# A hand-ordered attention and gMLP kernel: 50 steps of its list in other places, twelve of them zero products of the warm-up

## The chip, the cores and the metric

The kernel runs on one core of a Trainium2 chip. The core has five queues that work side by side and are each strictly in order here: TensorE (PE in the profile, its weight loads PEld), VectorE (DVE), ScalarE (ACT), GpSimd (POOL) and SyncE (SP), which issues nearly all DMAs. The metric is the device time of one execution in microseconds (us); lower is better.

## The reference

Inputs are q, k and v of shape (8, 8, 576, 64): 8 batches, 8 heads, 576 positions, head size 64. First comes attention with a causal window of 64 positions, then a gMLP block with spatial gating on the heads laid side by side.

```
scores = q @ k^T / 8 ; keep 0 <= t - s < 64, else -1e9
attn   = softmax(scores) ; x = (attn @ v) as (8, 576, 512)
h      = relu(x @ w_in)                 # 512 -> 1024
u, v   = h[..., :512], h[..., 512:]
v_n    = (v - mean(v)) / sqrt(var(v) + 1e-6)
v_s    = w_spatial @ v_n + b_spatial    # over the 576 positions
out    = (u * v_s) @ w_out              # 512 -> 512
```

## The kernel before, in words

All work is cut into 1111 named steps. A plan is first built: each step has a name, the engine that may run it, the buffers that it takes and the instructions that it issues. Then the string ORDER at the top of the file says in which order the steps are emitted, on which engine, and which buffer of its kind each one takes: `S0_0:PE:0:1` is step S0_0 on TensorE with score tiles 0 and 1. The function `as_listed` reads it, and the last loop of the kernel emits it. Since every engine's queue is in order, the places in ORDER are the order of each queue; across engines only semaphores for data and buffers hold a step back. A step that takes a buffer waits until the last readers of the step that had it are done.

The names, with b a batch, g a half of the heads (0 or 1), u a quarter, j or i a block of rows or columns:

- ldk, ldq, ldv (L401, L422), ldwin (L327), ldwsp (L343), ldb, ldwo: loads, issued by SyncE (DQ in the list). Loads of v come in five pieces (ldv2_03 is piece 3 of batch 2, half 0). There are 8 buffers for k, q and weights ("nat") and 4 for v ("natv").
- ck, cq, cv, sl, su, s4, cwin, cwsp, cb, cwo: casts to 16 bits and copies (L293 on ScalarE, L296, L299 and L301 on VectorE and GpSimd).
- tk, tq: 32 x 32 transposes on VectorE (L408).
- S (64 small matmuls, L470; S*_r, the last 64 positions, L539): scores into the two score tiles. Each S takes both. E (L477, L549): their exponential on ScalarE. M (L480, L553): the window's mask, a minimum on VectorE.
- Z (L493, L562): row sums; N and n (L519, L521): their logarithm and its negative exponential on ScalarE, so the inverse. P (L504, L575): attn @ v. X (L512, L583): product of both on VectorE, which gives x.
- V (L653, L666): the half of h that is normalised; Vr (L633) its relu, Vb (L635) and Va (L637) its statistics on VectorE, L1 and L2 (L680, L682) on ScalarE, A (L692) the normalised v_n on VectorE.
- U (L708, L713) and Ur (L721): the other half and its relu. W and We: transposes of w_spatial through TensorE, once, which need all five ldwsp.
- G (L738, L744) and Ge (L752): spatial product and gate. O (L763, and L669 within V*_4 of the next batch): product with w_out. Oe (L610): copy out of PSUM on ScalarE. st (L619, L626 and others): stores, in SyncE's queue too.
- D0 to D24 (L791): 25 steps of two matmuls each of a zeroed tile with itself into a bank that nobody reads. They have no data to wait for after the tile has been zeroed.

```
for _ in range(2):
    nc.tensor.matmul(m.t[:, :], scratch[:, 0:128], scratch[:, :], start=True, stop=True)
add(f"D{i}", ("PE", 0.43), -2.0, emit_D, acq=[m], mode="f")
```

TensorE has two score tiles of two PSUM banks each and four single banks, 0 to 3, which all other matmul steps take. The batches overlap: while the gMLP of batch b runs, the attention of batch b + 1 and the loads of b + 2 and b + 3 are under way. Before the first S stand eight D steps; the other 17 lie between the steps of the first attention, up to P0_11.

Of the kernel before, what the change touches and what calls it, by code (L numbers as in the profile page):

```python
# [42 lines left out]
Ur0_0:ACT:4 cv1_01:POOL W3:PE:1 We0:DVE ldv1_14:DQ sl1_00:ACT:2 We2:DVE ldk2_1:DQ:4 W4:PE:0
s41_0:ACT su1_00:DVE We3:ACT sl1_01:POOL W1:PE:2 su1_01:POOL A0_2:DVE:2 We4:ACT Z1_r:PE:3 P1_01:PE:1
A0_1:DVE:3 N1_r:ACT:0 We1:DVE ck2_0:POOL:0 ldwo10:DQ:5 P1_00:PE:0 Z1_10:PE:3 X1_00:DVE:2 G0_4:PE:2
ldq2_1:DQ:7 N1_10:ACT:4 G0_3:PE:0 n1_01:ACT X1_01:DVE tk2_0:DVE:2 cv1_10:POOL:3 ldwo00:DQ:6
n1_10:ACT sl1_10:ACT:3 G0_0:PE:3 su1_10:POOL cq2_0:ACT:1 ldwo11:DQ Ge0_3:DVE:0 G0_2:PE:1 ldwo01:DQ
Ge0_4:DVE:1 tq2_0:DVE:3 cv1_11:POOL ldq3_0:DQ:0 G0_1:PE:0 ldv2_00:DQ:0 s41_1:POOL sl1_11:ACT
su1_11:POOL n1_r:ACT Ge0_2:DVE:2 P1_10:PE:2 n1_11:ACT X1_10:DVE:3 ck2_1:POOL:2 P1_11:PE:1
ldk3_0:DQ:2 S2_0:PE:1:0 X1_11:DVE cwo10:ACT ldv2_01:DQ P1_r:PE:2 Ge0_0:DVE:3 V1_2:PE:1 E2_00:ACT:0  # L50
X1_r:DVE:1 Ge0_1:DVE:4 E2_01:ACT:1 V1_1:PE:3 cq2_1:POOL:3 ldv2_02:DQ tk2_1:DVE:0 V1_3:PE:2
Vr1_2:ACT:5 ldv2_03:DQ cwo00:POOL Vr1_1:ACT:6 tq2_1:DVE:1 U1_2:PE:0 ldv2_10:DQ:1 Vr1_3:ACT:7
cwo11:ACT ldv2_11:DQ V1_0:PE:1 M2_00:DVE Ur1_2:ACT:5 Vb1_2:DVE:5 cwo01:ACT S2_1:PE:1:0 Vr1_0:ACT:4
M2_01:DVE Z2_00:PE:3 cq3_0:POOL:0 ldv2_04:DQ E2_10:ACT:3 V1_4:PE:2 Vb1_1:DVE:1 ldv2_12:DQ Va1_2:DVE
Vb1_3:DVE:3 U1_1:PE:0 Vr1_4:ACT:2 M2_10:DVE Oe0_4:ACT:0 O0_0:PE:1 ck3_0:POOL:1 ldv2_13:DQ
Vb1_4:DVE:0 E2_11:ACT:2 Vb1_0:DVE:2 ldq4_0:DQ:3 O0_2:PE:2 Oe0_0:ACT:0 Va1_3:DVE ldv2_14:DQ Va1_4:DVE
Va1_1:DVE Ur1_1:ACT:0 Va1_0:DVE S2_r:PE:1:0 M2_11:DVE Z2_10:PE:1 cv2_00:POOL:1 ldv3_00:DQ:2
L11:ACT:1 O0_1:PE:0 tq3_0:DVE:4 L21:ACT Oe0_2:ACT:1 ldq3_1:DQ:1 N2_10:ACT:3 U1_4:PE:2 ldk3_1:DQ:4
A1_4:DVE E2_r0:ACT:0 U1_0:PE:1 N2_00:ACT:5 A1_0:DVE:4 ldv5_10:DQ:3 A1_2:DVE:5 Ur1_4:ACT:3 A1_1:DVE:6
U1_3:PE:3 Oe0_1:ACT A1_3:DVE:7 sl2_00:ACT:0 su2_00:POOL tk3_0:DVE:5 G1_1:PE:2 Ur1_3:ACT:1  # L60
# [13 lines left out]
O1_3:PE:0 n3_00:ACT ldk4_1:DQ:6 sl3_00:POOL:3 ldv4_00:DQ:1 Oe1_2:ACT:1 Va2_4:DVE Va2_2:DVE Va2_1:DVE
U2_1:PE:3 tk4_0:DVE:0 Ur2_3:ACT:1 su3_00:POOL L12:ACT:0 O1_0:PE:2 L22:ACT Oe1_3:ACT A2_4:DVE
s43_0:POOL A2_1:DVE:0 Ur2_1:ACT:3 O1_1:PE:1 ldv4_10:DQ:2 A2_3:DVE:1 s43_1:ACT ldk5_0:DQ:0 A2_0:DVE:2
Oe1_0:ACT:0 Z3_10:PE:0 A2_2:DVE:3 ldv4_11:DQ P3_00:PE:3 N3_10:ACT:3 P3_10:PE:2 ldq5_0:DQ:2
X3_00:DVE:2 S4_0:PE:1:0 ldv4_01:DQ Oe1_1:ACT M3_r:DVE ldv4_02:DQ G2_4:PE:0 ck4_1:ACT:0 ldv4_03:DQ
G2_2:PE:3 ldv5_11:DQ Ge2_4:DVE:1 E4_00:ACT:0 ldv4_04:DQ tk4_1:DVE:1 G2_3:PE:1 E4_01:ACT:3
ck5_0:POOL:1 ldk5_1:DQ:1 Ge2_2:DVE:0 ldv4_12:DQ Z3_11:PE:0 n3_10:ACT Ge2_3:DVE:2 Z3_r:PE:3  # L80
S4_1:PE:1:0 N3_r:ACT:4 X3_10:DVE:3 N3_11:ACT:2 P3_11:PE:1 M4_01:DVE n3_r:ACT P3_01:PE:3 cq5_0:POOL:3
ldv4_13:DQ P3_r:PE:2 n3_11:ACT G2_0:PE:0 X3_r:DVE:1 E4_10:ACT:2 ldq5_1:DQ:3 X3_01:DVE st1_1:DQ
X3_11:DVE G2_1:PE:2 E4_11:ACT:1 Ge2_0:DVE:3 ldv5_00:DQ:0 V3_3:PE:3 ldv5_01:DQ Ge2_1:DVE:4 st1_0:DQ
M4_00:DVE V3_1:PE:1 Vr3_3:ACT:5 M4_10:DVE Z4_01:PE:0 Vr3_1:ACT:6 M4_11:DVE V3_4:PE:2 ck5_1:POOL:2
N4_01:ACT:1 tk5_0:DVE:4 Z4_10:PE:3 Vr3_4:ACT:7 Z4_00:PE:1 S4_r:PE:1:0 Oe2_4:ACT:0 V3_2:PE:0
cv4_00:POOL:1 Vb3_1:DVE:2 N4_10:ACT:0 Vb3_3:DVE:4 U3_0:PE:2 E4_r0:ACT:0 sl4_00:POOL:0 Vr3_2:ACT:4
N4_00:ACT:3 U3_2:PE:3 Vb3_2:DVE:5 cq5_1:POOL:0 Ur3_0:ACT:5 tq5_0:DVE:5 V3_0:PE:0 su4_00:ACT
s44_0:POOL U3_4:PE:1 Va3_2:DVE cv4_10:POOL:0 Vr3_0:ACT:2 ldv6_10:DQ:1 O2_2:PE:2 ldv5_12:DQ
Ur3_2:ACT:4 Vb3_0:DVE:1 ldv4_14:DQ Ur3_4:ACT:2 U3_1:PE:0 Vb3_4:DVE:0 ldv5_02:DQ E4_r1:ACT
Oe2_2:ACT:1 ldv5_03:DQ Va3_3:DVE Va3_0:DVE P4_01:PE:3 Va3_1:DVE Va3_4:DVE ldq6_1:DQ:4 M4_r:DVE  # L90
# [751 lines left out]
```

## Time and profile before

| what | value |
|---|---|
| runs, us | 202.72, 202.97, 202.5 (median 202.72) |
| span of the profiled execution | 201.0 us |
| the profiled execution's own time beside its span | not given apart from the runs |
| TensorE busy | 188.6 us, 94% |
| VectorE, ScalarE, GpSimd busy | 161.2, 167.0, 76.5 us |
| mean granted TensorE clock | 0.996 |
| DMA | 42.69 MB, 212 GB/s on average |

A row of the timeline has its start, its length (of several instructions of one kind in a row, to the end of the last), engine, line, operation, destination and sources, shapes and count; in brackets the idle time ahead of it and what ended that. A row of the chain of waits has start, length and what the end of the program hung on at that time. A row of the windows has the stretch, its length, then the busy time of TensorE, its weight loads, VectorE, ScalarE and GpSimd with the number of instructions, the granted clock, the DMA engines' share and GB/s.

### The profile page before, as it was taken

The numbers are of one execution on the slowest core, as the hardware profiler recorded it, in microseconds if no ns is written. First come the engines' busy times: TensorE is split into PE (matmuls) and PEld (weight loads), VectorE is DVE, ScalarE is ACT, GpSimd is POOL, SyncE is SP. The second block draws the span as 40 slices with busy tenths as digits, with TensorE's granted clock in tenths as the row PEclk, the third lists the DMA queues.
The fourth block names the chain that finished last, engine by engine and source line by source line (L and its number), as shares of the span: only waits on it lengthen the run. The fifth ranks groups of instructions, "written<-read, shape, count | busy, mean of one in ns | idle before, by whom it ended". The sixth has DMA issues, their size and how long they took to land.

```text
span 201.0 us, 7008 instructions
## 1 busy us (share of the span) xinstructions
PE 188.6 (94%) x2927; PEld 97.7 (49%) x2927; DVE 161.2 (80%) x307; ACT 167.0 (83%) x307; POOL 76.5 (38%) x144
## 2 busy tenths in 40 slices
...
GB/s 221 387 276 184 336 378 210 292 372 377 185 274 255 246 221 188 295 243 234 311 118 262 241 316 178 227 284 249 185 111 117 3 5 132 108 0 0 128 145 202
DMA packets 50275, 42.69 MB, mean 212 GB/s; under 512 B 39361, under 2 KB 39489, under 8 KB 50242
## 3 DMA queue, kind: packets, MB, share of 16 engines
...
q8 instruction: 23, 0.38, 0.8%
q10 hardware_dynamic: 224, 0.33, 0.5%
...
## 4 chain that ended last, share of the span: by engine, by line
PE 70%; DMA 9%; SPq 7%; ACT 5%; DVE 5%; POOL 1%; issue 1%; POOLq 0%
PE bank L738 16%; PE bank L653 12%; PE bank L763 12%; PE bank L708 10%; DMA nk<-in_k_dram 9%; SPq L422 4%; PE pair L470 4%; PE bank L504 3%; PE bank L666 3%; PE bank L493 3%; PE bank L744 2%; SPq L327 2%; ACT e L477 1%; PE bank L713 1%; ACT ob L610 1%
## 5 line engine op out<-in xcount | busy, mean ns | idle before, releaser
L738 PE MATMUL bank<-wspT,vn 128*128 128x512 f16 (+1 forms) x160 | 37.5, 379 | 0.0
L477 ACT ACTIVATE e<-pair 128x1024 f16<-128x1024 f32 x32 | 31.9, 1027 | 2.7 <-PE pair L470 2.5
L752 DVE TENSOR_TENSOR g<-bank,ru 128x512 f16<-128x512 f32 (+1 forms) x40 | 24.8, 632 | 11.0 <-PE bank L738 5.0
L708 PE MATMUL bank<-x,win 128*128 128x512 f16 x128 | 31.6, 379 | 0.0
L763 PE MATMUL bank<-wout,g 128*128 128x512 f16 x128 | 31.3, 379 | 0.0
L653 PE MATMUL bank<-win,x 128*128 128x512 f16 x128 | 30.4, 379 | 0.2 <-DVE x L512 0.2
L721 ACT ACTIVATE ru<-bank 128x512 f32<-128x512 f32 (+1 forms) x40 | 21.4, 562 | 8.4 <-PE bank L708 4.6
L635 DVE BATCH_NORM_STATS2 st<-vs 128x6 f32<-128x512 f16 (+1 forms) x40 | 25.9, 670 | 3.0 <-ACT vs L633 2.8
L512 DVE TENSOR_TENSOR x<-bank,lz 128x512 f16<-128x512 f32 x32 | 21.2, 683 | 5.4 <-PE bank L504 2.6
L633 ACT ACTIVATE vs<-bank 128x512 f16<-128x512 f32 (+1 forms) x40 | 22.9, 597 | 3.1 <-PE bank L653 2.3
L610 ACT COPY ob<-bank 128x512 f32<-128x512 f32 (+1 forms) x39 | 22.6, 588 | 3.3 <-PE bank L763 3.1
L738 PEld LDWEIGHTS <-vn 128*128 128x128 f16 (+1 forms) x160 | 14.9, 97 | 17.7 <-DVE vn L692 0.5
L480 DVE TENSOR_TENSOR e<-e,mask 128x1024 f16<-128x1024 f16 x32 | 22.5, 721 | 1.0 <-ACT e L477 1.0
L408 DVE STREAM_TRANSPOSE qT<-hq 128x576 f32<-128x576 f32 x16 | 19.7, 1243 | 2.5 <-POOL hq L296 2.3
L296 POOL CAST hq<-nq 128x384 f16<-128x384 f32 x33 | 16.5, 536 | 13.1 <-DMA nq<-in_q_dram 12.5
L408 DVE STREAM_TRANSPOSE kT<-hk 128x576 f32<-128x576 f32 x16 | 20.0, 1247 | 1.4 <-ACT hk L293 1.1
L519 ACT ACTIVATE lz<-bank 128x512 f32<-128x512 f32 x32 | 18.6, 603 | 2.1 <-PE bank L493 2.0
L521 ACT ACTIVATE lz<-lz 128x512 f32<-128x512 f32 x32 | 19.6, 631 | 0.1
L653 PEld LDWEIGHTS <-x 128*128 128x128 f16 x128 | 12.0, 97 | 14.3 <-issue 0.6
L708 PEld LDWEIGHTS <-win 128*128 128x128 f16 x128 | 11.9, 98 | 14.4 <-issue 1.3
L763 PEld LDWEIGHTS <-g 128*128 128x128 f16 x128 | 11.8, 98 | 13.4 <-issue 0.5
L692 DVE TENSOR_SCALAR vn<-vs,mv,ln 128x512 f16<-128x512 f16 (+1 forms) x40 | 15.4, 436 | 3.5 <-ACT ln L682 3.3
...
## 6 DMA issues: line engine op xcount, KB each, us to landing
...
```

What stands on the lines that cost most here:

```text
L408: d = add(f"t{name}{b}_{g}", ("DVE", 1.09), key, lambda e: nc.vector.transpose(qt.t[:, :].rearrange("p (i j) -> p j i", j=18), h.t[:, :].b ...
L477: ex = add(f"E{b}_{g}{u}", ("ACT", 0.91), key, lambda e, u=u: nc.scalar.activation(e2[u].t[:, :, :], sc[u].t[:, :, :], AF.Exp, bias=0.0, s ...
L480: mins.append(add(f"M{b}_{g}{u}", ("DVE", 0.65), key, lambda e, u=u: nc.vector.tensor_tensor(e2[u].t[:, :, :], e2[u].t[:, :, :], mask[:, : ...
L610: lambda e: (nc.vector.tensor_copy if last else nc.scalar.copy)(view(), m.t[rows, 0:n]),
L633: rl = add(f"Vr{b}_{j}", ("ACT", 0.49), key, lambda e: nc.scalar.activation(vs.t[0:jn, :], m.t[0:jn, :], AF.Relu), deps=[pv], acq=[vs], us ...
L635: s1 = add(f"Vb{b}_{j}", ("DVE", 0.6), key + 0.02, lambda e: nc.vector.bn_stats(st6.t[0:jn, 0:6], vs.t[0:jn, :]), deps=[rl], acq=[st6], us ...
L653: nc.tensor.matmul(m.t[:, :], xr(b, r)[:, 128 * j:128 * j + 128], w_in_sb[r][:, 512:1024], start=(r == 0), stop=(r == 3))
L708: nc.tensor.matmul(m.t[:, :], w_in_sb[r][:, 128 * i:128 * i + 128], xr(b, r), start=(r == 0), stop=(r == 3))
L721: lambda e, m=m, ru=ru, n=n: nc.scalar.activation(ru.t[:, 0:n], m.t[:, 0:n], AF.Relu), deps=[pu], acq=[ru], uses=[m])))
L738: nc.tensor.matmul(m.t[:, :], w[0:kn, 128 * i:128 * i + 128], wspT[kk][0:kn, 0:512], start=(kk == 0), stop=(kk == 4))
L752: lambda e, m=m, g=g, ru=ru, n=n: nc.vector.tensor_tensor(g.t[:, 0:n], m.t[:, 0:n], ru.t[:, 0:n], ALU.mult),
L763: nc.tensor.matmul(m.t[:, :], G[r][0].t[:, 128 * j:128 * j + 128], w_out_sb[r][:, :], start=(r == 0), stop=(r == 3))
```

## The change

The steps are the same, each on the same engine; 50 of them stand in other places, and the numbers of banks and buffers are dealt out anew along the list.

- TensorE: 19 D steps instead of 8 stand ahead of S0_0. D24, D13 and D19 come between S0_0 and S0_1 (before: D21, D7, D11, D24), D2, D4 and D3 between S0_1 and S0_r (before: five), and none behind S0_r (before: eight). All but the first four use bank 0. Z1_10 goes ahead of P1_00, P2_00 behind S3_0, P3_10 ahead of Z3_10, V3_0 ahead of U3_2, Z4_r ahead of P4_00, and G3_4 from behind P4_r to ahead of Z4_11.
- VectorE: Va0_1 goes from behind Va0_3 to ahead of tq1_1; Vb0_4 ahead of Va0_3; M2_11 from ahead of tq3_0 to behind tk3_0; M2_r ahead of X2_00; Va3_3 and Va3_1 ahead of Vb3_0; Ge3_4 from behind X4_11 to ahead of Ge3_1; Va4_2 ahead of Va4_4.
- ScalarE: Oe0_1, Vr3_0, Ur3_1 (now behind L23), Oe2_3, sl4_10 and n4_r (now ahead of Ur3_3), sl6_10, n5_10 and N2_01.
- GpSimd: cv2_10 ahead of su2_00, cq4_1 ahead of cq4_0, s43_0 ahead of su3_00.
- Transfers: ldwsp4 ahead of ldwsp1; ldv2_03 and ldv2_04 behind ldv2_13; ldq4_0 later and ldq4_1 earlier; ldv5_10 from ahead of ldv3_10 to ahead of st1_4; st0_1 from ahead of st0_4 to behind ldv3_04; ldv5_11, ldv4_13 later; ldv6_00 and ldv6_11 around st2_4.
- Buffers: ldv3_10 takes v buffer 3 instead of 0, ldv5_10 buffer 0 instead of 3; ldwsp4 takes nat buffer 6, ldwsp1 buffer 2, ldwsp0 buffer 0 (before: 0, 6, 2).

The core of the diff, its first hunk; the rest of ORDER changes in the same way, and since bank numbers follow, nearly every line of it does.

```diff
-ldk1_0:DQ:5 ldv0_10:DQ:1 D15:PE:3 cq0_0:POOL:0 ldv0_11:DQ D22:PE:0 D6:PE:1 tq0_0:DVE:0 D0:PE:2
-ck0_0:ACT:1 ldv0_01:DQ D16:PE:3 tk0_0:DVE:1 ck0_1:ACT:2 ldv0_02:DQ S0_0:PE:0:1 tk0_1:DVE:2 D21:PE:0
-E0_00:ACT:0 ldv0_12:DQ D7:PE:1 D11:PE:2 cq0_1:DVE:3 E0_01:ACT:1 ldv0_03:DQ D24:PE:3 tq0_1:DVE:3
-M0_01:DVE cq1_0:ACT:0 ldwin100:DQ:6 S0_1:PE:0:1 M0_00:DVE D5:PE:0 E0_10:ACT:2 tq1_0:DVE:4 D17:PE:1
-D2:PE:2 ldv0_04:DQ E0_11:ACT:3 D4:PE:3 ck1_0:DVE:1 ldv0_13:DQ D1:PE:0 S0_r:PE:0:1 M0_10:DVE
-ldv0_14:DQ Z0_00:PE:1 E0_r0:ACT:0 cv0_10:DVE:0 Z0_10:PE:2 E0_r1:ACT M0_11:DVE ldwin110:DQ:7
-Z0_01:PE:3 N0_10:ACT:0 D10:PE:0 sl0_10:DVE:0 cv0_00:DVE:1 N0_01:ACT:1 ldb:DQ:0 M0_r:DVE N0_00:ACT:2
-sl0_00:DVE:1 Z0_r:PE:2 su0_00:DVE ldwin111:DQ Z0_11:PE:0 N0_r:ACT:3 D9:PE:3 n0_00:ACT cv0_01:DVE
-ldwin101:DQ D8:PE:1 su0_01:DVE sl0_01:POOL n0_10:ACT su0_10:DVE D13:PE:2 ldwin000:DQ:1 n0_01:ACT
-tk1_0:DVE:5 s40_0:POOL ldk1_1:DQ:2 N0_11:ACT:4 P0_01:PE:3 ldq1_1:DQ:3 P0_00:PE:1 n0_11:ACT
-cv0_11:DVE ldwin001:DQ S1_0:PE:0:1 sl0_11:DVE X0_00:DVE:0 D20:PE:2 cwin110:POOL ldwin010:DQ:4
-E1_00:ACT:1 s40_1:DVE D19:PE:0 ldwin011:DQ su0_11:POOL X0_01:DVE ldwsp3:DQ:5 E1_01:ACT:0 M1_00:DVE
-cwin111:POOL P0_10:PE:1 P0_11:PE:2 X0_10:DVE:1 D18:PE:0 cwin100:ACT cwin101:POOL ldwsp2:DQ:7 D3:PE:3
-n0_r:ACT X0_11:DVE cwin000:ACT Z1_00:PE:1 M1_01:DVE ldwsp1:DQ:6 P0_r:PE:0 cb:ACT V0_1:PE:3
-X0_r:DVE:0 V0_2:PE:2 ck1_1:POOL:2 ldwsp4:DQ:0 Vr0_1:ACT:0 N1_00:ACT:5 Vb0_1:DVE:0 V0_0:PE:0
-Vr0_2:ACT:1 tk1_1:DVE:0 cq1_1:POOL:3 ldv1_00:DQ:2 V0_3:PE:3 Vr0_0:ACT:2 n1_00:ACT ldwsp0:DQ:2
-Z1_01:PE:1 tq1_1:DVE:1 V0_4:PE:2 cwin001:ACT cwin010:POOL ldv1_01:DQ N1_01:ACT:2 cwin011:POOL
+ldk1_0:DQ:5 ldv0_10:DQ:1 D15:PE:3 cq0_0:POOL:0 ldv0_11:DQ D22:PE:0 D6:PE:0 tq0_0:DVE:0 D0:PE:0
+ck0_0:ACT:1 D9:PE:0 ldv0_01:DQ D16:PE:0 tk0_0:DVE:1 D1:PE:0 D17:PE:0 ck0_1:ACT:2 ldv0_02:DQ D7:PE:0
+D11:PE:0 D18:PE:0 D5:PE:0 tk0_1:DVE:2 D10:PE:0 D21:PE:0 D8:PE:0 D20:PE:0 S0_0:PE:0:1 E0_00:ACT:0
+ldv0_12:DQ cq0_1:DVE:3 E0_01:ACT:1 ldv0_03:DQ D24:PE:0 tq0_1:DVE:3 M0_01:DVE cq1_0:ACT:0 D13:PE:0
+ldwin100:DQ:6 D19:PE:0 S0_1:PE:0:1 M0_00:DVE E0_10:ACT:2 tq1_0:DVE:4 D2:PE:0 ldv0_04:DQ E0_11:ACT:3
+D4:PE:0 D3:PE:0 ck1_0:DVE:3 ldv0_13:DQ S0_r:PE:0:1 M0_10:DVE ldv0_14:DQ Z0_00:PE:0 E0_r0:ACT:0
+cv0_10:DVE:0 Z0_10:PE:1 E0_r1:ACT M0_11:DVE ldwin110:DQ:7 Z0_01:PE:2 N0_10:ACT:0 sl0_10:DVE:0
+cv0_00:DVE:1 N0_01:ACT:1 ldb:DQ:0 M0_r:DVE N0_00:ACT:2 sl0_00:DVE:1 Z0_r:PE:3 su0_00:DVE ldwin111:DQ
+Z0_11:PE:1 N0_r:ACT:3 n0_00:ACT cv0_01:DVE ldwin101:DQ su0_01:DVE sl0_01:POOL n0_10:ACT su0_10:DVE
+ldwin000:DQ:1 n0_01:ACT tk1_0:DVE:5 s40_0:POOL ldk1_1:DQ:2 N0_11:ACT:4 P0_01:PE:2 ldq1_1:DQ:3
+P0_00:PE:0 n0_11:ACT cv0_11:DVE ldwin001:DQ S1_0:PE:0:1 sl0_11:DVE X0_00:DVE:0 cwin110:POOL
+ldwin010:DQ:4 E1_00:ACT:1 s40_1:DVE ldwin011:DQ su0_11:POOL X0_01:DVE ldwsp3:DQ:5 E1_01:ACT:0
+M1_00:DVE cwin111:POOL P0_10:PE:3 P0_11:PE:1 X0_10:DVE:1 cwin100:ACT cwin101:POOL ldwsp2:DQ:7
+ck1_1:POOL:1 ldwsp4:DQ:6 n0_r:ACT X0_11:DVE cwin000:ACT Z1_00:PE:0 M1_01:DVE ldwsp1:DQ:2 P0_r:PE:2
+cb:ACT V0_1:PE:3 X0_r:DVE:0 V0_2:PE:1 Vr0_1:ACT:0 N1_00:ACT:5 Vb0_1:DVE:0 V0_0:PE:2 Vr0_2:ACT:1
+tk1_1:DVE:0 cq1_1:POOL:2 ldv1_00:DQ:2 Va0_1:DVE V0_3:PE:3 Vr0_0:ACT:2 n1_00:ACT ldwsp0:DQ:0
+Z1_01:PE:0 tq1_1:DVE:1 V0_4:PE:1 cwin001:ACT cwin010:POOL ldv1_01:DQ N1_01:ACT:2 cwin011:POOL
 Vr0_3:ACT:3 ldv1_02:DQ Vb0_2:DVE:1 S1_1:PE:0:1 Vr0_4:ACT:4 Vb0_0:DVE:2 cwsp3:POOL ldv1_03:DQ
...
-E2_r1:ACT ldv3_10:DQ:0 Ge1_0:DVE:6 s42_1:ACT P2_00:PE:1 Z2_11:PE:2 su2_10:POOL ldv3_11:DQ
-V2_1:PE:0 cv3_10:POOL:2 Oe0_3:ACT Vb2_0:DVE:4 P2_r:PE:2 st0_1:DQ Vr2_1:ACT:2 Z3_00:PE:1 X2_r:DVE:0
+Ge1_1:DVE:5 n2_00:ACT sl2_10:POOL:1 s42_0:ACT Z2_01:PE:0 E2_r1:ACT ldv3_10:DQ:3 Ge1_0:DVE:6
+su3_10:POOL ldv3_03:DQ E3_10:ACT:3 ldv3_14:DQ G1_2:PE:2 ldv3_04:DQ ck4_0:POOL:1 tq4_0:DVE:3 st0_1:DQ
...
```

More of the change, by code (lines that the diff above doesn't have):

```diff
@@ L43 @@
[L43 to L60, printed above, removed]
@@ L73 @@
-Ur2_4:ACT:4 cv3_00:POOL:3 Oe1_4:ACT:0 O1_2:PE:2 Vb2_2:DVE:0 n3_01:ACT st1_4:DQ Va2_3:DVE Vb2_4:DVE:1
[L74 to L90, printed above, removed]
@@ L91 @@
-Ur3_1:ACT:1 P4_00:PE:1 tq5_1:DVE:0 ldv5_13:DQ S5_0:PE:1:0 L13:ACT:1 n4_00:ACT Z4_r:PE:2 L23:ACT
-O2_0:PE:0 N4_r:ACT:4 A3_3:DVE:4 n4_01:ACT X4_00:DVE:0 O2_1:PE:2 E5_01:ACT:3 A3_0:DVE:5 A3_1:DVE:6
-A3_4:DVE U3_3:PE:1 Oe2_0:ACT:0 A3_2:DVE:7 Oe2_1:ACT M5_01:DVE O2_3:PE:0 E5_00:ACT:0 X4_01:DVE
-G3_0:PE:2 tk5_1:DVE:1 Ur3_3:ACT:0 n4_10:ACT G3_3:PE:3 M5_00:DVE n4_r:ACT Oe2_3:ACT sl4_10:ACT:1
-su4_10:POOL G3_1:PE:1 Ge3_3:DVE:8 Ge3_0:DVE:5 s44_1:POOL Z4_11:PE:0 Z5_01:PE:3 Ge3_1:DVE:6
-cv5_00:POOL:2 ldv6_00:DQ:2 N4_11:ACT:5 P4_10:PE:2 S5_1:PE:0:1 ldv5_04:DQ X4_10:DVE:1 N5_01:ACT:2
```

171 lines of the change are left out of this document (106 added, 65 removed).

## The prediction

> **What bounds the kernel now.** I read the page first, then the chain that ended last, then the timeline of the first 31 us engine by engine, then windows, because most moved steps lie early. No separate time is given for the profiled execution: its span is 201.0 us and the median of the three runs is 202.72 us (202.5 to 202.97). The 1.7 us between them are taken as fixed, and every change below is added to 202.72. A difference of 0.2% is 0.4 us, about what a measurement of this kernel can tell from none.
>
> ```profile
> span 201.0 us, 7008 instructions
> PE 188.6 (94%) x2927; PEld 97.7 (49%) x2927; DVE 161.2 (80%) x307; ACT 167.0 (83%) x307; POOL 76.5 (38%) x144
> ```
>
> ```profile
> 19.27 6.71 DMA nk<-in_k_dram
> 26.10 1.41 POOL hk L296 x3
> 27.51 1.39 POOL hq L296 x3
> 28.92 1.27 DVE qT L408
> 30.23 0.81 PE pair L470 x46
> ```
>
> ```profile
> 39.91 0.76 PE bank L744 x20
> ```
>
> TensorE is busy 94% of the span, and from 40 us on the chain is nearly all TensorE. So a delay that reaches G0_4 at 39.91 is carried to the end unless TensorE later gives back a stall. The chain's early part is a load (ldk1_1, issued at 19.27), its casts on GpSimd, a transpose on VectorE (tq1_1) and S1_1 at 30.23. Here the zero products matter only by what waits behind them.
>
> ```profile
> 1.27 5.35 PE L791 MATMUL bank<-scratch 128*128 128x512 f16 x16 [1.27 <-DVE scratch L234]
> 8.67 0.76 PE L470 MATMUL pair<-qT,kT 32*64 32x128 f16 x64 [2.05 <-DVE kT L408]
> 9.37 1.90 PE L791 MATMUL bank<-scratch 128*128 128x512 f16 x8
> 9.48 1.94 ACT L477 ACTIVATE e<-pair 128x1024 f16<-128x1024 f32 x2 [0.52 <-PE pair L470]
> 10.88 1.26 DVE L408 STREAM_TRANSPOSE qT<-hq 128x576 f32<-128x576 f32 x1
> 11.99 1.26 DVE L480 TENSOR_TENSOR e<-e,mask 128x1024 f16<-128x1024 f16 x2
> 12.20 0.77 PE L470 MATMUL pair<-qT,kT 32*64 32x128 f16 x64 [0.93 <-DVE qT L408]
> 20.49 0.77 PE L470 MATMUL pair<-qT,kT 32*64 32x128 f16 x64 [0.57 <-DVE kT L408]
> ```
>
> ```profile
> L791 PE MATMUL bank<-scratch x50: 379/379/634, 1.3 to 23.4; 128*128 128x512 f16 x50
> ```
>
> ```profile
> 12.00:25.60 13.60, 11.93 (x277) 6.25 (x278) 13.47 (x27) 11.34 (x20) 3.68 (x6) 1.00 0.95 254
> ```
>
> The reader should see two things. Before S0_0 TensorE is free for 2.05 us; and from 12.0 to 25.6 VectorE is busy 13.47 of 13.60 us, so in that stretch VectorE has no slack, while TensorE has plenty.
>
> **Part 1: eleven more zero products ahead of S0_0.** Before, eight D steps (16 matmuls, two each) stand ahead of S0_0 and end at 1.27 + 5.35 = 6.62. Now 19 stand there, 38 matmuls. The 22 more run at the pace of the x8 row: (1.90 - 0.38) / 7 = 0.217 us each, where 0.38 is the median of one such matmul (379 ns in the row of L791); 22 x 0.217 = 4.77. The last of them is out of the way at 6.62 - 0.38 + 4.77 + 0.217 = 11.2, against S0_0's 8.67: 2.5 us late. Bounds: all 38 at 0.217 would give 9.5; all at the mean pace of the first 16 (5.35 / 16 = 0.33) would give 14.0. I take 11.2, because the first 16 hold whatever the slow start costs.
>
> E0_00 and E0_01 follow S0_0 by 0.81 (9.48 - 8.67) and take 1.94, so they end at 13.95 instead of 11.42. M0_01 needs them; it started at 11.99, straight behind tq0_1, and now starts at about 14.0. That is 2.0 us late on VectorE, whose queue is in order: tq1_0, ck1_0, all cv, sl and su copies of batch 0, X0_* and M1_* stand behind it, and there is no idle time to take it up before 25.6. S0_1 needs the same score tiles and starts at 14.0, 1.8 late. The eight D steps that stood behind S0_r free nothing: P0_01, S1_0 and Z1_00 waited for VectorE and GpSimd, not for them.
>
> ```profile
> 24.57 0.62 ACT L293 CAST win<-wi 128x512 f16<-128x512 f32 x1 [0.50 <-DMA wi<-in_moe_w_in_dram]
> 25.21 0.67 ACT L293 CAST wspT<-wsb 1x576 f16<-1x576 f32 x1
> 25.91 0.60 ACT L633 ACTIVATE vs<-bank 128x512 f16<-128x512 f32 x1
> 25.22 0.41 DVE L583 TENSOR_TENSOR x<-bank,lz_r 128x256 f16<-128x256 f32 x1
> 26.54 0.69 DVE L635 BATCH_NORM_STATS2 st<-vs 128x6 f32<-128x512 f16 x1 [0.90 <-ACT vs L633]
> 27.54 1.26 DVE L408 STREAM_TRANSPOSE kT<-hk 128x576 f32<-128x576 f32 x1 [0.31 <-POOL hk L296]
> 28.92 1.26 DVE L408 STREAM_TRANSPOSE qT<-hq 128x576 f32<-128x576 f32 x1
> ```
>
> Between X0_r and tq1_1 VectorE has its first idle time: 0.90 + 0.31 + 0.12 (28.92 - 28.80). The last two wait for the casts at 26.10 and 27.51, which hang on a load that does not move. The 0.90 waits for Vr0_1 on ScalarE, which was held by cwin000's DMA wait (0.50) and cb. ScalarE is 1.85 late there, less that 0.50: Vr0_1 ends at 27.85 instead of 26.51. X0_r ends at 27.63, Vb0_1 starts at 27.85, and with tk1_1, Va0_1 (moved in ahead of tq1_1, about 0.1) and tq1_1 (31.05 instead of 30.18) 0.85 is left of the 2.0. The later queue no longer holds Va0_1, so M1_11 and all behind it, to We1 and G0_4, are **0.75 us late**. ldwsp4 and ldwsp1 change places and SyncE now stands at ldwsp1 until ck1_1 has been cast (27.51); behind it wait ldv1_00 and ldwsp0, which have some time in hand. Taken at nothing: W0, which needs all five ldwsp, is itself 0.75 later. If that cover is gone it costs some tenths.
>
> **Part 2: the clock.** With no D step behind S0_r, TensorE is nearly idle from about 16 to 26 us. The rows that come nearest:
>
> ```profile
> 18.44:21.85 3.41, 2.84 (x104) 1.74 (x102) 3.36 (x8) 2.88 (x6) 1.87 (x4) 1.00 0.86 274
> 195.93:199.35 3.42, 1.17 (x11) 0.46 (x9) 0.42 (x1) 0.96 (x2) 0.00 (x0) 1.00 0.82 293
> 199.00:200.98 1.98, 0.00 (x0) 0.00 (x0) 0.00 (x0) 0.00 (x0) 0.00 (x0) 0.59 0.20 49
> ```
>
> At the end the granted clock fell to half: a mean of 0.59 over 1.98 us is 0.36 us at full and the rest at half, so the fall came at 199.36, after 3.4 us in which TensorE was busy 1.17. In the kernel before, the stretch of that length from 18.44 holds 2.84 busy and keeps the clock. Without its zero products that stretch holds Z0_r, Z0_11, P0_01 and P0_00 alone, some 0.9 to 1.2 us, like the one that lost the clock. The other end is the 2.05 us idle before S0_0, which did not lose it; the longest single gap would now be about 1.5 us. I put the fall at a little over one half. Its price: S1_0, whose 0.70 issue time would double, delays E1_00 and through it M1_00 on the full VectorE queue: **+0.7**. The least is 0; the most is that V0_1 to V0_4 run at half too (four groups of 0.86, half hidden by the late VectorE): +2.0. I take +0.7, as S1_0's own row has it.
>
> [...]
>
> **Part 3: the loads of 57 to 78 us.**
>
> ```profile
> 57.48 5.84 SPq L422 DMA_DIRECT2D nv<-in_v_dram  x4
> 71.41 0.39 SPq L626 DMA_DIRECT2D out_dram<-ob  x1
> ```
>
> ```profile
> 78.62 5.78 DMA nk<-in_k_dram
> 87.44 0.30 PE bank L562 x4
> ```
>
> ```profile
> 86.47 0.41 PE L493 MATMUL bank<-e,ones 128*64 128x512 f16 x2
> 82.88 0.58 ACT L610 COPY ob<-bank 128x512 f32<-128x512 f32 x1
> 84.42 1.15 ACT L293 CAST hk<-nk 128x1152 f16<-128x1152 f32 x1 [0.96 <-DMA nk<-in_k_dram]
> ```
>
> The largest stall of TensorE after 40 us is here: Z3_11 at 86.47 needs 0.22, Z3_r starts at 87.44, so 0.75 is lost. Z3_r's bank waits for Ge2_2, that stands on VectorE behind tk4_1, that waits for ck4_1, and that for ldk4_1, which lands 5.78 us after its issue. In the order of before, SyncE stood twice: four issues (ldv5_10 and the first three of ldv3_1) spread over the 5.84 us from 57.48, since ldv3_10's buffer was still read, and then it stood at st0_1, which waits for Oe0_3, until 71.41. So ldv3_02 to ldv3_04 and st0_0 came after 72, not long ahead of ldk4_1. Now ldv3_10 takes another buffer and st0_1 stands behind the loads: the queue is empty when ldk4_1 is issued. If it lands 1 us sooner, ck4_1 starts when ScalarE is free (Oe1_1 ended at 83.46, plus the delay) and the 0.75 is given back. Bounds: 0 to 0.96; I take **-0.75**. ldv2_03 and ldv2_04 go behind four other loads, which makes cv2_00 1.5 us later on GpSimd; su2_10, moved behind su2_00, then ends about 1 us later, as P2_10 does: nothing.
>
> **Part 4: the rest.** M2_11, M2_r, Va and Vr moves, V3_0 ahead of U3_2, Z4_r, P3_10, P2_00, Z1_10, the GpSimd swaps and Ur3_1 behind L23: around nearly all of them TensorE has no gap, so they can gain nothing there. G3_4 ahead of Z4_11 adds Ge3_4 and a later Ur3_3 ahead of Ge3_1 and X4_10:
>
> ```profile
> 60.00:70.00 10.00, 10.00 (x188) 5.53 (x187) 8.93 (x15) 9.14 (x17) 4.10 (x9) 1.00 0.86 250
> 90.00:100.00 10.00, 10.00 (x98) 4.72 (x97) 8.37 (x14) 8.49 (x15) 5.39 (x13) 1.00 0.95 278
> 100.00:110.00 10.00, 10.00 (x159) 5.17 (x158) 9.67 (x21) 9.11 (x20) 6.47 (x12) 1.00 0.73 179
> ```
>
> ```profile
> 111.58 0.42 DVE L583 TENSOR_TENSOR x<-bank,lz_r 128x256 f16<-128x256 f32 x1 [0.73 <-PE bank L575]
> 115.71 0.24 PE L539 MATMUL pair<-qT,kT 32*64 32x64 f16 x9 [0.50 <-issue]
> ```
>
> The 0.73 idle takes up most of it; P4_10's bank now waits for Ge3_4: 0 to 0.2, taken as +0.1. The 0.50 stall inside S5_r waits for nothing that the profile shows; I leave it as it is.
>
> Sum: +0.75 + 0.7 - 0.75 + 0.1 = +0.8, so **203.5 us**, slower.
>
> **The rivals.** (1) The clock stays: +0.1, 202.8 us, no change that can be told. For it speaks the 2.05 us gap that was survived, against it the tail. (2) Faster: the clock stays, Z3_r's 0.75 and S5_r's 0.50 both go, and the 2.0 on VectorE is absorbed down to 0.5 because S0_0 comes out 0.3 sooner: 0.5 - 0.75 - 0.5 = -0.75, 202.0 us. It decides at S0_0: below about 11.0 with full clock the early loss is smaller than what the loads give back. Against it: S5_r's stall has no cause that the change touches. (3) Much slower: half clock lasts through V0 (+2.0 in place of 0.7), or S0_0 comes at 12 and nothing is given back at Z3_r: +1.5 to +2.1, 204.2 to 204.8 us. (4) The change does not do what it says: not possible for the D steps, since TensorE issues in order.
>
> **How the numbers follow.** Forecast 0.42 (its own range 203.1 to 204.0), rival 1 0.24, rival 2 0.18, rival 3 0.16. Faster by over 0.4 us is rival 2 and a little of the first: 0.20. Within 0.4 us is most of rival 1: 0.22. The rest is slower: 0.58. The range goes from a little under rival 2 to a little over rival 3, since S0_0's bounds are wide: 201.9 to 204.9.
>
> **What would show it.** S0_0 at 11.2, M0_01 at 14.0 with some 1.9 us idle on VectorE ahead of it, S1_1 near 31 to 31.8, a granted clock below 1 somewhere in 18 to 27 us, no wait of ScalarE for ldk4_1 and no stall ahead of Z3_r. The forecast is wrong if S0_0 starts before 10, if G0_4 is less than 0.3 late, or if new stalls of TensorE appear after 40 us.

## The result, and the profile after

| | before | after |
|---|---|---|
| median, us | 202.61 (202.48 to 202.97, 4 runs) | 208.2 (206.75 to 209.3, 4 runs) |
| profiled execution, us; its span | not given apart; 201.0 | 208.18; 206.5 |
| mean granted TensorE clock | 0.996 | 0.972 |

The ratio is 1.0276 (95% interval 1.0216 to 1.0335): 2.8% slower, where 203.5 us and a range of 201.9 to 204.9 had been forecast. In this and every comparison below, executions over 1.5% above the fastest of the same kernel are left out; where a kernel's clock falls in some executions and not in others this drops its dearest ones, so below such kernels have their executions listed with the clock that each was granted.

The head of the page after, with the clock in 40 slices of 5.2 us:

```profile
span 206.5 us, 7014 instructions
PE 193.6 (94%) x2927; PEld 100.7 (49%) x2927; DVE 163.7 (79%) x307; ACT 166.5 (81%) x307; POOL 76.8 (37%) x144
PEclk9999559999999999999999999999999999999998
```

The work and its counts are the same, but TensorE's busy time has grown by 5.0 us. About 4 of them, an estimate, lie in the fifth and sixth slice: the three stretches at half clock below hold 8.04 us of busy time, which would be about half at the full clock (a zero product took 0.43 us ahead of the full clock's start at 7.21 us in this trace, and 0.22 behind it). Windows of the kernel after, cut where its clock changes (length; busy time and count of TensorE, weight loads, VectorE, ScalarE, GpSimd; granted clock; DMA share; GB/s):

```profile
14.04:17.45 3.41, 2.95 (x75) 1.42 (x74) 2.17 (x3) 3.41 (x5) 0.00 (x0) 1.00 0.98 197
17.45:20.86 3.41, 1.60 (x45) 0.80 (x46) 3.40 (x10) 2.78 (x6) 0.00 (x0) 1.00 0.76 203
20.87:24.28 3.41, 2.09 (x74) 1.63 (x77) 3.30 (x8) 3.17 (x7) 1.83 (x4) 0.50 1.00 319
24.28:27.69 3.41, 2.54 (x95) 2.10 (x80) 3.13 (x7) 2.73 (x5) 3.34 (x6) 0.50 1.02 373
27.69:31.10 3.41, 3.41 (x9) 1.21 (x8) 2.17 (x5) 2.28 (x5) 3.30 (x7) 0.50 1.03 316
```

A stretch of 3.41 us with 1.60 us of work ends in a fall to half. Two more at half hold 2.09 and 2.54 us and do not bring the clock back; the fourth is full and does. So three stretches, 10.24 us, run at half.

The timeline after: the zero products, S0_0, S1_0 and the four V steps from V0_1 to V0_3 on TensorE, the same V steps before, and G0_4 after; then VectorE's first two M steps and first Vb step after.

```profile
1.27 11.30 PE L791 MATMUL bank<-scratch 128*128 128x512 f16 x38 [1.27 <-DVE scratch L234]
12.49 0.77 PE L470 MATMUL pair<-qT,kT 32*64 32x128 f16 x64
23.81 1.08 PE L470 MATMUL pair<-qT,kT 32*64 32x128 f16 x64 [0.57 <-DVE kT L408]
27.54 5.37 PE L653 MATMUL bank<-win,x 128*128 128x512 f16 x16
```

```profile
24.62 3.63 PE L653 MATMUL bank<-win,x 128*128 128x512 f16 x16
```

```profile
45.00 0.76 PE L744 MATMUL bank<-wspT,vn 128*128 128x64 f16 x20 [0.59 <-DVE wspT L301]
15.28 1.29 DVE L480 TENSOR_TENSOR e<-e,mask 128x1024 f16<-128x1024 f16 x2 [3.33 <-ACT e L477]
30.10 0.70 DVE L635 BATCH_NORM_STATS2 st<-vs 128x6 f32<-128x512 f16 x1 [1.25 <-ACT vs L633]
```

S0_0 starts 3.82 us late (12.49 against 8.67), M0_01 3.29 late, V0_1 to V0_3 take 1.74 us longer, and G0_4 is 5.09 late (45.00 against 39.91). The chain of waits of the kernel after (start, length, what it hung on) shows V0 as one long piece of TensorE, then ScalarE for 2.8 us (left out here) and VectorE up to G0_4, where before it had hung on a load and GpSimd's casts:

```profile
23.81 1.16 PE pair L470 x56
...
27.61 4.45 PE bank L653 x12
...
36.42 0.76 DVE e L480
...
43.54 0.94 DVE vn L692 x2
...
45.00 0.76 PE bank L744 x20
```

### The profile page after: what moved, and what is told of

The parts are those of the page before. It is cut to its first block, busy times and chain, and to the rows that moved or that the text cites. A ratio compares the mean times of both kernels' runs of the same rounds, so it can differ in the third digit from the quotient of the medians.

```text
span 206.5 us, 7014 instructions
## 1 busy us (share of the span) xinstructions
PE 193.6 (94%) x2927; PEld 100.7 (49%) x2927; DVE 163.7 (79%) x307; ACT 166.5 (81%) x307; POOL 76.8 (37%) x144
## 4 chain that ended last, share of the span: by engine, by line
PE 72%; DVE 8%; ACT 7%; SPq 4%; DMA 4%; issue 3%; DVEq 0%
PE bank L738 17%; PE bank L653 13%; PE bank L763 13%; PE bank L708 9%; PE pair L470 4%; SPq L422 4%; PE bank L493 3%; PE bank L504 3%; PE bank L666 3%; PE bank L744 3%; DMA nk<-in_k_dram 2%; DMA nv<-in_v_dram 2%; PE bank L713 1%; ACT ob L610 1%; ACT vs L633 1%
## 5 line engine op out<-in xcount | busy, mean ns | idle before, releaser
L653 PE MATMUL bank<-win,x 128*128 128x512 f16 x128 | 32.2, 395 | 0.2 <-DVE x L512 0.2
L708 PE MATMUL bank<-x,win 128*128 128x512 f16 x128 | 31.8, 379 | 0.0
L480 DVE TENSOR_TENSOR e<-e,mask 128x1024 f16<-128x1024 f16 x32 | 24.5, 784 | 4.6 <-ACT e L477 4.6
L296 POOL CAST hk<-nk 128x384 f16<-128x384 f32 x27 | 15.1, 592 | 18.9 <-DMA nk<-in_k_dram 15.6
L653 PEld LDWEIGHTS <-x 128*128 128x128 f16 x128 | 12.4, 101 | 15.6 <-issue 2.8
L692 DVE TENSOR_SCALAR vn<-vs,mv,ln 128x512 f16<-128x512 f16 (+1 forms) x40 | 16.0, 450 | 3.6 <-ACT ln L682 3.5
```

The costliest lines, as they stand in the source:

```text
L296: nc.gpsimd.tensor_copy(o[:, n:n + 384], i[:, n:n + 384])
L480: mins.append(add(f"M{b}_{g}{u}", ("DVE", 0.65), key, lambda e, u=u: nc.vector.tensor_tensor(e2[u].t[:, :, :], e2[u].t[:, :, :], mask[:, : ...
L653: nc.tensor.matmul(m.t[:, :], xr(b, r)[:, 128 * j:128 * j + 128], w_in_sb[r][:, 512:1024], start=(r == 0), stop=(r == 3))
L708: nc.tensor.matmul(m.t[:, :], w_in_sb[r][:, 128 * i:128 * i + 128], xr(b, r), start=(r == 0), stop=(r == 3))
```

## The experiments

The theory after the result: the loss is all in the 25 D steps, and mainly in the clock that falls because none of them is left behind S0_r. Rivals: the other moves cost it, or S0_0's late start does by itself. Four numbers such as 19 / 3 / 3 / 0 tell how many D steps stand ahead of S0_0, between S0_0 and S0_1, between S0_1 and S0_r, and behind S0_r; before it is 8 / 4 / 5 / 8.

**1. Only the D steps (e1_warm_only).** The kernel before with its D steps 19 / 3 / 3 / 0.

```diff
-... D0:PE:2 ... D16:PE:3 ... S0_0:PE:0:1 ... D21:PE:0 ... D7:PE:1 D11:PE:2 ...
+... D0:PE:0 D9:PE:0 D16:PE:0 D1:PE:0 ... D8:PE:0 D20:PE:0 S0_0:PE:0:1 ...
```

> The order of before, with the 25 zero products alone in their new places (19 ahead of S0_0, three and three, none behind S0_r); all else as before. Theory 1 (the zero products carry all of the loss: S0_0 comes late behind them, and with none behind S0_r the granted clock falls to half): 207 to 209 us, S0_0 at 11.2 to 12.5, half clock for two or three stretches of 3.4 us between 18 and 31 us, G0_4 late by 4 to 5 us. Theory 2 (the other moves cost most of it): 202.6 to 204.5 us.

207.82 us (206.81 to 208.27, 4 runs), ratio 1.0264 (1.0215 to 1.0313). The D steps alone give the whole loss. S0_0 is at 12.27, the clock is at half from 20.41 to 30.65, and then once more:

```profile
17.00:20.41 3.41, 1.66 (x40) 0.59 (x38) 3.41 (x9) 2.78 (x6) 0.00 (x0) 1.00 0.64 185
...
40.89:44.30 3.41, 2.17 (x49) 1.60 (x49) 3.35 (x9) 2.63 (x6) 3.22 (x6) 1.00 0.88 285
44.30:47.72 3.42, 3.34 (x26) 1.93 (x26) 2.48 (x4) 3.42 (x8) 2.03 (x5) 0.50 0.99 336
```

**2. Everything but the D steps (e2_rest_only).** The changed kernel with its D steps back at 8 / 4 / 5 / 8.

```diff
-... D21:PE:0 D8:PE:0 D20:PE:0 S0_0:PE:0:1 ...
+... D6:PE:1 D0:PE:2 D16:PE:3 S0_0:PE:0:1 ... D10:PE:3 Z0_r:PE:3 ... D18:PE:0 D3:PE:2 Z1_00:PE:0 ...
```

> The changed order, with the 25 zero products back where they stood among the steps of before (8 ahead of S0_0, 4, 5, and 8 behind S0_r); everything else as changed. Theory 1: no fall of the clock, G0_4 near 39.9, and the stall ahead of Z3_r (0.75 us before) gone, so 201.8 to 202.8 us. Theory 2: 205 to 208 us.

202.9 us (202.16 to 205.02, 10 runs), ratio 1.0051 (1.0009 to 1.0094). The other moves together are 0.1 to 0.9% slower, not faster. In the profile S0_0 is at 8.67, as before; the clock never falls before the end.

**3. The change plus eight D steps behind S0_r (e3_after_plus8).**

```diff
-NWARM = 25
+NWARM = 33
-... Z0_r:PE:3 ... P0_01:PE:2 ...
+... D25:PE:3 Z0_r:PE:3 ... D26:PE:2 D27:PE:0 D28:PE:3 P0_01:PE:2 ...
```

> The changed kernel with eight more zero-product steps (33 in all), which stand behind S0_r where before had its eight. S0_0 stays late, the clock has its work. Theory 1, both halves: the clock holds 1.0 to the end and what is left is the late S0_0, 1 to 2 us at G0_4, so 203.3 to 204.6 us. If the late S0_0 alone is the cause and the clock's fall only goes with it: 207 to 209 us. If the fall alone is the cause: 202 to 203 us.

208.18 us (204.79 to 209.56, 4 runs), without a ratio. By execution, with the mean clock: 0.998 208.33 (the profiled one) and 204.79; 0.997 208.03; 0.992 209.56. So three of the four took as long as the changed kernel although the clock held, which fits what was expected of the late S0_0 alone; only the profile speaks against that reading. In it the clock is full from 4.53 us to the end, S0_0 is at 11.16, M0_01 at 13.95, S1_1 at 31.37 (1.1 late) and G0_4 at 40.81 (0.9 late). This part is what the prediction had worked out, and 4 us better at G0_4 than the changed kernel. The other 4.6 us are lost after 88 us at places with full clock, the two largest a gap of 1.61 us within G2_0 at 90 us and one M step of 4.53 us at 116; what stood beside them is told in experiment 5 and at the end. Where the other three executions lost their time was not seen.

```profile
91.99 1.91 PE L739 MATMUL bank<-wspT,vn 128*128 128x512 f16 x8 [1.61 <-issue]
116.16 4.53 DVE L481 TENSOR_TENSOR e<-e,mask 128x1024 f16<-128x1024 f16 x1
```

**4. The kernel before without its eight D steps behind S0_r (e4_before_minus8):** 8 / 4 / 5 / 0.

```diff
-NWARM = 25
+NWARM = 17
-... D10:PE:0 ... Z0_r:PE:2 ... D9:PE:3 ... D8:PE:1 ... D13:PE:2 ... P0_01:PE:3 ... D20:PE:2 ... D19:PE:2 ... D18:PE:0 ... D3:PE:3
+... Z0_r:PE:2 ... P0_01:PE:3 ...
```

> The order of before without the eight zero-product steps behind S0_r (17 in all, the others in their places), so S0_0 stays at 8.7. Theory 1: the clock falls to half between 15 and 22 us all the same and stays there for 7 to 10 us; 204 to 206.5 us. If the late S0_0 alone is the cause: clock at 1.0, 202.4 to 202.8 us.

204.78 us (202.07 to 206.35, 10 runs), ratio 1.007 (1.0016 to 1.0124). S0_0 is on time (8.83), the clock falls:

```profile
18.22:21.63 3.41, 1.55 (x98) 1.29 (x95) 3.33 (x7) 2.96 (x6) 1.89 (x4) 1.00 0.74 224
21.63:25.05 3.42, 1.83 (x50) 1.52 (x42) 3.42 (x8) 3.31 (x6) 2.21 (x3) 0.50 0.96 327
25.05:28.46 3.41, 3.41 (x13) 1.19 (x9) 1.55 (x4) 1.71 (x3) 2.04 (x5) 0.50 1.01 390
```

With two stretches at half, as in this profile, G0_4 is 1.1 late. The executions say the same: at a mean clock of 0.983 they took 203.14, 203.67 and 202.07 us; at 0.970 to 0.975, so with some 10 to 12 us or about three stretches at half, 204.17 to 206.19 (six of them); at 0.964, 206.35. The kernel before had a median of 202.56 beside them. So about three stretches at half cost 1.6 to 3.6 us with S0_0 on time, more than the profile with two shows.

**5. S0_0 late, eight D steps behind S0_r (f1_late_only).** The changed kernel with 17 / 0 / 0 / 8.

```diff
-... D24:PE:0 ... D13:PE:0 ... D19:PE:0 S0_1:PE:0:1 ... D4:PE:0 D3:PE:0 ... S0_r:PE:0:1 ...
+... S0_1:PE:0:1 ... S0_r:PE:0:1 ... D8:PE:3 Z0_r:PE:3 ... D20:PE:2 D24:PE:0 D13:PE:3 P0_01:PE:2 ...
```

> The changed kernel with its 25 zero-product steps dealt 17 / 0 / 0 / 8 (ahead of S0_0, between S0_0 and S0_1, between S0_1 and S0_r, behind S0_r) instead of 19 / 3 / 3 / 0, so S0_0 stays late, TensorE stays occupied behind S0_r, and no later instruction changes its number. The theory (the fallen clock is what is dear; a late S0_0 alone is mostly taken up by VectorE's first idle time): clock full from 4.5 or 7.2 us to the end, S0_0 between 10.3 and 11.7, G0_4 0.5 to 1.0 late, 203 to 204 us. The rival (the late S0_0 is what is dear): G0_4 3 or more late, 205.5 to 208 us.

206.26 us (205.18 to 207.72, 6 runs), ratio 1.0212 (1.0153 to 1.027): the time that the rival had expected, but in the one profiled not for its reason. Between S0_0 and S0_r nothing was left, so a stretch with 1.01 us of work came there and the clock fell once, earlier than before. And 2.5 us were lost at one place with the clock full, in the middle of Z1_00. The window, then Z1_00's two matmuls on TensorE and the weight loads behind them:

```profile
13.42:16.83 3.41, 1.01 (x66) 0.76 (x64) 2.72 (x4) 3.41 (x4) 0.00 (x0) 1.00 0.98 199
```

```profile
25.90 0.40 PE L493 MATMUL bank<-e,ones 128*64 128x512 f16 x1
28.40 0.38 PE L493 MATMUL bank<-e,ones 128*64 128x512 f16 x1 [2.10 <-issue]
28.41 0.39 PEld L575 LDWEIGHTS <-hs 128*64 128x64 f16 x8 [2.40 <-issue]
```

Two matmuls of one step stand 2.50 us apart, and the profile shows no wait for a semaphore between them. Counted from the start, the gap lies behind TensorE's instruction 705, with matmuls, weight loads and the two others at the start counted together. The queue that the page calls "q8 instruction" moved one packet of 16,384 bytes at that moment, from 25.94 us on; in the trace before, with the same instruction 705 at 24.16, that packet had come at 21.33. Until there this profile runs beside that of experiment 3 (S1_0 at 22.64 and 22.49). Take off the 2.5 us and G0_4, 3.32 late, would be 0.8 late; that is argued, and experiment 8 tests it. The executions with this clock (0.992) took 206.1, 205.97 and 206.42 us, one at 0.982 205.18, two at 0.975 207.72 and 207.31; whether all lost the time at this place was not seen.

**6. S0_0 on time, no D step behind S0_r (f2_none_behind):** the changed kernel with 8 / 8 / 9 / 0.

```diff
-... D20:PE:0 S0_0:PE:0:1 ...
+... D9:PE:0 S0_0:PE:0:1 ... S0_1:PE:0:1 ... S0_r:PE:0:1 ...
```

> The changed kernel with its zero-product steps dealt 8 / 8 / 9 / 0: S0_0 on time as in the kernel before, none behind S0_r. The theory: S0_0 at 8.7 to 8.9, the clock at half for two or three stretches of 3.4 us from some 21 us on, 203 to 206 us, the slower the more stretches (about 1 us for two, 2 to 3 for three). The rival (the late S0_0 is what is dear): within 0.5 us of the kernel before.

205.89 us (203.73 to 207.72, 6 runs), ratio 1.0148 (1.0085 to 1.021). S0_0 is at 8.56 and the clock falls for two stretches from 22.99 on, after this one:

```profile
19.58:22.99 3.41, 1.35 (x78) 1.04 (x76) 3.33 (x6) 3.38 (x8) 1.74 (x4) 1.00 0.94 304
```

One execution kept the clock (0.999): 203.73 us. At 0.983 it took 206.01, 205.38 and 205.77, so two stretches cost about 2 us here; at 0.975 and 0.970, so with about three, 207.72 and 207.12. That is not the price of a fall by itself: the nine D steps ahead of S0_r make S0_r 2.3 us late, which the expectation had not seen, so this kernel too has a delay and a fall.

**7. Four D steps behind S0_r, S0_0 on time (f3_four_behind):** 8 / 6 / 7 / 4.

```diff
+... D19:PE:3 Z0_r:PE:3 ... D2:PE:0 ... P0_01:PE:2 ... D4:PE:3 P0_10:PE:3 ... D3:PE:0 Z1_00:PE:0 ...
```

> The changed kernel with its zero-product steps dealt 8 / 6 / 7 / 4: S0_0 on time, and every second of the eight steps behind S0_r back in its place. It measures how much work keeps the clock. If about half a stretch busy is enough, the clock stays full and the time is within 0.5 us of the kernel before; if not, it falls as with none behind S0_r and the time is 203 to 206 us. I lean to the first, since four steps add 1.7 us to some 4 us of real work between 16 and 26 us.

204.27 us (202.8 to 206.07, 12 runs), ratio 1.0077 (1.0039 to 1.0116), within the noise of experiment 2, which has all eight. Four steps hold the clock: the thinnest stretch behind S0_r keeps 2.57 us of work, and no execution had a mean clock below 0.991, which leaves room for one stretch at half at most. The executions still lie 3.3 us apart; at 1.0 they took 203.3 to 206.07 us.

```profile
18.99:22.41 3.42, 2.57 (x122) 1.73 (x122) 3.37 (x7) 3.39 (x6) 2.05 (x4) 1.00 0.74 223
```

In this profile G0_4 is at 39.63, and TensorE's last step, O7_4, is 0.12 us later than before. No version that was run beats the kernel before.

**8. S0_0 late, four behind (g1_late_four_behind):** 17 / 2 / 2 / 4.

```diff
-... D24:PE:0 ... D13:PE:0 ... D19:PE:0 S0_1:PE:0:1 ... D2:PE:0 ... D4:PE:0 D3:PE:0 ... S0_r:PE:0:1 ...
+... S0_1:PE:0:1 ... S0_r:PE:0:1 ... D19:PE:3 Z0_r:PE:3 ... D3:PE:0 Z1_00:PE:0 ...
```

> The changed kernel with its zero-product steps dealt 17 / 2 / 2 / 4: S0_0 late (10.3 to 11.7), with just so many steps behind S0_r as kept the clock when S0_0 was on time. It repeats the run with 17 / 0 / 0 / 8, in whose profile one stall of 2.5 us, at the edge of a 16 KB block of TensorE's instructions, hid what the late S0_0 costs alone. If a late S0_0 alone is cheap: G0_4 0.5 to 1.2 late once stalls at such an edge are taken off, 203 to 204.5 us. If it is dear by itself: G0_4 2.5 or more late with the clock full and no such stall, 205.5 to 207 us.

204.32 us (202.94 to 210.79, 6 runs), ratio 1.0115 (1.0047 to 1.0184). The profile has what those of experiments 3 and 5 lacked, a late S0_0 alone, with the clock full from 5.68 to 200.24 us and no gap behind instruction 705 or a multiple of 256 further before 115 us. S0_0 and G0_4 on TensorE, M0_01 and tq1_1 on VectorE:

```profile
10.87 0.77 PE L470 MATMUL pair<-qT,kT 32*64 32x128 f16 x64
40.29 0.76 PE L744 MATMUL bank<-wspT,vn 128*128 128x64 f16 x20 [0.36 <-DVE wspT L301]
13.66 1.29 DVE L480 TENSOR_TENSOR e<-e,mask 128x1024 f16<-128x1024 f16 x2 [1.38 <-ACT e L477]
29.54 1.26 DVE L408 STREAM_TRANSPOSE qT<-hq 128x576 f32<-128x576 f32 x1
```

S0_0 is 2.20 late, M0_01 1.67, tq1_1 0.62, G0_4 0.38, O7_4 0.75. So a late S0_0 alone is cheap in this profile. Its stretches of 2.08 and 2.17 us of work between 15.92 and 22.75 kept the clock. By execution, with the mean clock: 0.998 204.49; 0.996 203.53; 0.991 205.66; 0.983 204.16 and 202.94; 0.982 210.79. Here the time does not go with the clock, and what made the last one so long was not seen.

**9. As the change, but four behind (g2_nineteen_four_behind):** 19 / 1 / 1 / 4.

```diff
-... D13:PE:0 ... D19:PE:0 S0_1:PE:0:1 ... D4:PE:0 D3:PE:0 ... S0_r:PE:0:1 ...
+... S0_1:PE:0:1 ... S0_r:PE:0:1 ... D19:PE:3 Z0_r:PE:3 ... D2:PE:0 ... D4:PE:3 ... D3:PE:0 Z1_00:PE:0 ...
```

> The changed kernel with its zero-product steps dealt 19 / 1 / 1 / 4: as many ahead of S0_0 as the change has, so S0_0 at 11.2 to 12.5 by when the clock comes up, but four behind S0_r. If the two faults add up and the clock's is the larger, it lies well below the changed kernel: G0_4 0.8 to 2 late, 203.5 to 205 us. If the late S0_0 is what is dear, it stays at 206.5 to 208 us.

206.1 us (202.91 to 209.38, 6 runs), ratio 1.0115 (1.0035 to 1.0195), by three of the six executions. All six, by mean clock: 0.992 202.91; 0.991 204.46; 0.983 205.55; 0.979 206.64; 0.975 207.93 and 209.38. One kernel thus gives a time near the forecast, with one stretch at half at most (0.008 of 201.2 us lost is 3.2 us at half), and the time of the changed kernel, and here the clock goes with it. That speaks against the rival of the late S0_0 by itself, which experiment 3 had left open: S0_0 is 2.80 late in the profile. Two of its stretches, with 1.93 and 1.97 us of work, hold little less than the 2.08 that kept the clock in experiment 8; the profile, the one at 0.979, lost it behind both:

```profile
15.38:18.80 3.42, 1.93 (x41) 0.81 (x40) 3.42 (x7) 2.79 (x5) 0.00 (x0) 1.00 0.76 187
...
39.28:42.69 3.41, 1.97 (x54) 1.59 (x54) 3.34 (x7) 2.75 (x6) 3.22 (x7) 1.00 1.07 373
42.69:46.10 3.41, 3.41 (x22) 1.54 (x19) 2.55 (x4) 3.41 (x7) 2.58 (x7) 0.50 1.04 402
```

## Why the prediction was wrong

The sign and the two mechanisms of the loss were right; the size was not, and a part of the loss had no term.

**The step that failed is part 2, the price of the clock.** That it falls was forecast a little over one half, by the right stretch: 0.9 to 1.2 us of work were expected there, 1.60 were measured. The price, +0.7, was put on one step, S1_0, whose time was to double. S1_0 took 1.08 instead of 0.77 us, and that cost nothing behind it: from S0_0 to V0_1 the delay shrinks by 0.90 us here (3.82 to 2.92) and by 0.91 in experiment 3 (2.50 to 1.59), where the clock stayed full. But the same paragraph calls TensorE nearly idle from 16 to 26 us, which is three stretches, not one, and at half the clock did not come back in a stretch with 2.54 us of work. The three carried the half clock through V0_1 to V0_3, which took 5.37 instead of 3.63 us: +1.74. That term stood there as the upper end, +2.0, "half hidden by the late VectorE" (half of its four groups of 0.86 would be 1.7). It was not hidden: V0_4 was 4.66 late, 2.92 and 1.74.

**The sum had no term for the rest.** Experiment 3 has the same D steps up to S0_r and kept the clock. Measured against it, the 5.09 us at G0_4 are 0.89 of the late S0_0, as in experiment 3; 1.33 because the full clock came later (part 1 below); 1.74 of V0; 0.40 less because TensorE's wait of 0.79 us ahead of S1_1 now takes up 0.86 and not 0.46; and 1.53 between S1_1 and G0_4, where the delay grows by 1.29 (3.80 to 5.09) and in experiment 3 shrinks by 0.24. VectorE's idle time of 0.90, 0.31 and 0.12 us, which in part 1 takes up 1.25 of 2.0 us, takes up little: Vb0_1 waits 1.25 us for the slow V0 (the row of 30.10) and starts 3.56 late, and tq1_1 is 2.91 late where experiment 8 has 0.62 and the forecast 0.85.

One at a time the two delays looked small in the profiles: 0.4 late at G0_4 in experiment 8, 1.1 in experiment 4. But S0_0 was only 2.20 late there, and only two stretches ran at half. Whether delays of equal size cost more together than the sum of both is therefore not shown.

From S1_1 to G0_4 VectorE stands on the chain, and its two M steps take 1.87 us where they took 1.25. GpSimd casts beside them as soon as a load has landed, from 36.04 on (36.62 before), and the delayed M steps now fall into that time. That GpSimd slows them is argued from these rows and was not tried: before, one GpSimd cast also ran beside the second of these M steps, which kept its 0.7 us. Two M steps on VectorE and two copies on GpSimd, after, and the same two M steps before:

```profile
36.34 1.87 DVE L480 TENSOR_TENSOR e<-e,mask 128x1024 f16<-128x1024 f16 x2
36.72 1.97 POOL L301 COPY hs<-hv 64x512 f16<-64x512 f16 x2
```

```profile
32.83 1.25 DVE L480 TENSOR_TENSOR e<-e,mask 128x1024 f16<-128x1024 f16 x2
```

**Part 1, S0_0 at 11.2:** it came at 12.49, inside the bounds, and cost 1.33 us more than put for it. The pace was right: with the clock full from 4.53 us on, experiment 3 has S0_0 at 11.16, M0_01 at 13.95 (forecast 14.0) and G0_4 0.89 late (0.75). What differed was the start of the full clock: 4.79 in the trace before, 7.21 in the one after, and zero products followed each other at 0.43 us ahead of it and at 0.22 behind it, in both traces, so that each microsecond by which it comes later costs about half a one: 11.2 + (7.21 - 4.79) / 2 = 12.4. The same sum gives 12.2 for experiment 1 and 11.4 for experiment 9, where 12.27 and 11.47 were measured. The start was read from one execution as if it were fixed; over the eleven profiles it lies anywhere from 4.5 to 7.2 (below).

**Part 3, -0.75 at Z3_r:** right. Z3_11 and Z3_r follow each other without a gap, and the cast of ldk4_1 on ScalarE waits for nothing:

```profile
91.88 0.41 PE L493 MATMUL bank<-e,ones 128*64 128x512 f16 x2
92.12 0.28 PE L562 MATMUL bank<-er,ones 128*64 128x128 f16 x4
89.01 1.17 ACT L293 CAST hk<-nk 128x1152 f16<-128x1152 f32 x1
```

From V2_2 to Z3_r the delay shrinks from 5.41 to 4.68 us. But it grows again by 0.3 up to G3_0, through short waits ahead of Z4_r and O2_0 (0.02 and 0.19 us) that the kernel before does not have and experiment 2 has as well, and is 5.47 at O7_4. So the gain is real, and the moves around it give at least a part of it back: by the times of experiment 2 they are together not faster.

**Part 4:** the move of G3_4 cost what was put for it (from G3_0 to S5_r the delay grows by 0.11; 0.1 was taken). The stall of S5_r that waits for nothing visible was left as it was; it became 0.73 instead of 0.50, and the section on the hardware tells which packet came beside it:

```profile
121.03 0.23 PE L539 MATMUL pair<-qT,kT 32*64 32x64 f16 x8 [0.73 <-issue]
```

Of the signs named beforehand, the clock and Z3_r came as said; S0_0, M0_01 (15.28) and S1_1 (34.04 instead of 31 to 31.8) did not.

**The rivals.** Rival 3 named the cause, half clock through V0 and S0_0 at 12, with a chance of 0.16. It put the two as alternatives, "or", where they came together, and so stopped at 204.8 us, which set the range. It had no term for VectorE behind S1_1 either. Rival 1 had the clock stay, and named for it the gap of 2.05 us ahead of S0_0 that was survived. In the trace after the clock fell, behind a stretch with 1.60 us of work. No stretch that lost it in the runs was idle: before the end of the program they held 1.01 to 2.17 us of work.
